# Gated MLP up to the token mix: from a fixed sequence after the planner to planned groups of four token tiles

## Chip, core, metric

One core of one Trainium2 chip. The metric is device time in microseconds (us), the median of the runs. The engines are TensorE (PE), VectorE (DVE), ScalarE (ACT), GpSimd (POOL) and SyncE (SP), which here issues nearly all DMAs. Each engine runs its instructions in the order in which the program emits them.

## What is computed

S = 2048 tokens, D = 640, Fh = 864, all in bfloat16. Cut to what matters:

```python
sa, ca, ga, sb, cb, gb = split(silu(c) @ w_mod)          # six rows of 640
h  = layernorm(x) * (1 + ca) + sa                        # x = A_q
kv = shift_conv(A_k, shift_k) * A_v                      # 4 taps
y  = irfft(rfft(kv, 2S) * rfft(ssm_k, 2S))[:S] + kv * ssm_D
x  = x + ga * (h * y)
h  = layernorm(x) * (1 + cb) + sb
z  = gelu(h @ w_in);  z1, z2 = z[:, :Fh], layernorm(z[:, Fh:])
g  = w_sp @ z2 + b_sp[:, None]                           # token mix, 2048 x 2048
out = x + gb * ((z1 * g) @ w_out)
```

## The kernel before

**Long convolution.** It is done as a transform by matrix products. The 640 channels are cut into four units (`UNITS`, L25: 128, 192, 192, 128 wide). For each unit the filter (`K`) and the data (`U`) are loaded as `X`, go through a first small transform (`stage1`, L377, PE then an ACT copy into `X1`), and then through 16 frequency blocks: the forward transform `pu` (L398; for the filter ACT copies it to `KH`, L415), the product `T` on DVE (L426), the inverse `pz` (L430, six matmuls) and an ACT copy into `Z` (L443). A block's tables are `M2` (forward; POOL, DVE and ACT sine, L318) and `G2` (inverse; PE transposes of `M2` and copies, L346). When a unit's `Z` is whole, it is transposed into `ZT`, by DMA (L602) or, for the last unit, on PE (L608). Then `py` (L573) gives `y`, which DVE multiplies into `gh`, the normalised and modulated `x` (L588, L592). `resid` (L626) adds `gh` to `xt` in four groups of four token tiles and takes the row statistics `st2`, per unit.

**Data.** `kv` is made strip by strip: two DMA transposes for `k` and `v` (`load_kv`, L452), four taps on PE, a DVE product (L485), and a store to `kv_scr` in DRAM (L488), from which a unit's `X` is loaded (L368). The modulation rows come through 18 loads `wm` (L522), with two buffers. POOL does `gh_mod` (L560), the residual adds of the first three units, and reciprocal roots (L193).

**Order.** All of this is recorded as operations with costs, dependencies and a wanted step `t` (`Plan`, L36). `run` (L60) repeatedly takes the operation that can start first by its cost model, among equals the one with the smallest `t`, and emits it. `SLOTS` (L33) gives the buffers of each tag; a DMA holds SP for its modelled transfer and lands `LAND` ns later. The steps `t` are written by hand in each call.

**MLP.** It is emitted after the planner, when the transform's pools are closed: `prep` (aggregate, root), `norm` (`xn`), `flip` (PE transposes of `xn`, modulated into `h2T`), 32 `z2` accumulations (L758) with Gelu on ACT and statistics on DVE, then 28 for `z1T` (L790), the normalisation of `z2` (L798), the token mix over all 16 tiles of `z2` (L809) and the output product (L821). `wT`, the transposed `w_sp`, is loaded by 16 DMA transposes (L715) into memory that `gh` and the transform's tiles held.

Of the kernel before, what the change touches and what calls it, by code (L numbers as in the profile page):

```python
# [10 lines left out]
ALU = mybir.AluOpType  # L11
# [18 lines left out]
WS = ((0, 256), (256, 256), (512, 128))  # L30
HOP = 150
LAND = 2000
SLOTS = dict(X=3, X1=3, KH=17, T=4, Z=2, ZT=2, wm=2, big=2, dg=2, st1=2, ga=1, s1=2, pu=3, pz=2, py=1)  # L33


class Plan:  # L36
# [6 lines left out]
    def op(self, eng, fn, r=(), w=(), t=0.0, new=()):  # L43

        i = len(self.ops)
        deps = set()
# [10 lines left out]
        self.ops.append(dict(eng=eng, fn=fn, deps=deps, t=t, new=new))  # L57
        return i

    def run(self, engines):  # L60
# [14 lines left out]
        held = {}  # L75
# [17 lines left out]
        while len(order) < len(ops):  # L93
            best = None
            for i in ready:
# [4 lines left out]
                for e, cost in o["eng"].items():  # L100
# [3 lines left out]
                    key = (max(at, free[e]), o["t"], i)  # L104
# [4 lines left out]
            (at, _, _), i, e, cost = best  # L109
# [5 lines left out]
            done[i] = at + cost + (LAND if e == "SP" else 0)  # L115
# [10 lines left out]
def kernel(  # L126
# [70 lines left out]
    w_in = {}  # L197
    with ExitStack() as actx:
        consta = actx.enter_context(tc.tile_pool(name="consta", bufs=1))
        gh = consta.tile([P, NT, D], BF16)  # L200
        M2 = consta.tile([P, 3, NKC, P], BF16)
        G2 = consta.tile([P, 4, NKC, P], BF16)
# [12 lines left out]
        rstd1 = consta.tile([P, NT], F32)  # L215
        F1flat = F1bd[:].rearrange("p j g -> p (j g)")
# [3 lines left out]
        tl = {}  # L220
# [3 lines left out]
        def new(name, tag, shape, dtype=BF16, pool=None):  # L224
            if pool is None:
                pool = psA if tag in ("s1", "pu", "pz", "py") else bigp if tag == "big" else apool
# [48 lines left out]
        def f1_table():  # L275
# [16 lines left out]
                gmask[:, None, :].to_broadcast([P, NJ, 8]), op=ALU.mult), w=["F1"], t=-50)  # L292


        def e_table():
            t = -4
# [3 lines left out]
            def angles(e):  # L300
# [17 lines left out]
        def m2_chunk(i):  # L318
            t = -34 + 2 * i
# [43 lines left out]
        def load_X(name, src, u, t, r=()):  # L363
# [491 lines left out]
```

## Time and profile before

| | |
|---|---|
| median of 3 runs | 378.61 us (378.11 to 378.89) |
| the profiled execution | 379.7 us, of which span 377.7 us |
| first inverse matmul, last inverse matmul | 44.53, 159.1 us |
| first `z2` matmul, first mix matmul | 181.5, 247.1 us |
| mean granted TensorE clock | 0.977 |

The span goes from the first to the last instruction. In a row of the timeline stand start, duration, engine, line, operation, out<-in and count, and in brackets the idle time ahead of it and what ended it. In a group's row stand count, busy time, mean ns, idle time ahead. A row of DMA issues ends with the median us from issue to landing. Several matmuls in one row overlap, so a row's duration holds one latency beside the array's own time. "SPq" is SP's DMA queue.

### The profile page before, as it was taken

The numbers are of one execution on the slowest core, as the hardware profiler recorded it, in microseconds if no ns is written. First come the engines' busy times: TensorE is split into PE (matmuls) and PEld (weight loads), VectorE is DVE, ScalarE is ACT, GpSimd is POOL, SyncE is SP. The second block draws the span as 40 slices with busy tenths as digits, with TensorE's granted clock in tenths as the row PEclk, the third lists the DMA queues.
The fourth block names the chain that finished last, engine by engine and source line by source line (L and its number), as shares of the span: only waits on it lengthen the run. The fifth ranks groups of instructions, "written<-read, shape, count | busy, mean of one in ns | idle before, by whom it ended". The sixth has DMA issues, their size and how long they took to land.

```text
span 377.7 us, 6095 instructions
## 1 busy us (share of the span) xinstructions
PE 331.1 (88%) x2394; PEld 203.7 (54%) x2394; DVE 228.6 (61%) x497; ACT 150.8 (40%) x318; POOL 113.8 (30%) x117
## 2 busy tenths in 40 slices
PE   1388699899999999821999999999999999999996
PEld 0136575668667788720555544444444444446774
DVE  7769899566737988897777669012333233234553
ACT  4467356858598586430766655510000000000000
POOL 8942320583829579062200078000000000000000
PEclk9999999999999999985799999999999999999999
DMA  9869929398995669705999901000000000000222
GB/s 122 240 150 218 247 81 192 122 203 140 169 239 116 159 185 194 112 0 109 222 233 191 256 2 24 4 2 0 4 12 0 14 2 0 0 2 29 86 82 83
DMA packets 112708, 40.08 MB, mean 106 GB/s; under 512 B 97992, under 2 KB 111912, under 8 KB 112680
## 3 DMA queue, kind: packets, MB, share of 16 engines
q1 hardware_dynamic: 111184, 39.18, 48.8%
q0 software_dynamic: 192, 0.52, 0.7%
q8 instruction: 18, 0.29, 0.3%
q10 hardware_dynamic: 1304, 0.00, 0.2%
q14 instruction: 10, 0.08, 0.1%
HBM read 16.63 MB, written 5.24 MB: 58 GB/s over the span
## 4 chain that ended last, share of the span: by engine, by line
PE 56%; DMA 3%; DVE 3%; issue 3%; POOL 1%; ACT 1%; ACTq 0%; DVEq 0%; POOLq 0%
PE ps L809 26%; PE ps L821 8%; PE ps L790 8%; PE ps L758 7%; PE pz L231 3%; DMA ZT<-Z 2%; PE pu L231 2%; PE tp L746 1%; DVE xn L740 1%; DMA wm<-in_w_mod_dram 1%; PE s L231 1%; POOL xt L630 1%; DVE st L633 1%; DVE T L426 1%; PE py L231 0%
## 5 line engine op out<-in xcount | busy, mean ns | idle before, releaser
L809 PE MATMUL ps<-wT,z 128*128 128x512 bf16 (+1 forms) x448 | 96.9, 379 | 0.0
L809 PEld LDWEIGHTS <-z 128*128 128x128 bf16 (+1 forms) x448 | 45.4, 101 | 51.3
L812 DVE TENSOR_TENSOR gt<-ps,bsp 128x512 bf16<-128x512 f32 (+1 forms) x28 | 19.3, 691 | 75.2 <-PE ps L809 75.2
L426 DVE TENSOR_TENSOR T<-pu,KH 128x512 bf16<-128x512 f32 (+1 forms) x64 | 50.6, 817 | 16.5 <-PE pu L231 9.2
L231 PE MATMUL pu<-X,M 128*128 128x128 bf16 (+3 forms) x384 | 49.8, 254 | 0.7 <-ACT KH L415 0.7
L231 PE MATMUL pz<-T,G 128*128 128x192 bf16 (+3 forms) x384 | 45.4, 255 | 3.1 <-DVE T L426 2.8
L393 ACT CAST X<-s 128x512 bf16<-128x512 f32 x80 | 43.9, 592 | 6.6 <-PE s L231 5.8
L231 PEld LDWEIGHTS <-G 128*128 128x128 bf16 x384 | 32.5, 98 | 10.6 <-issue 4.1
L231 PEld LDWEIGHTS <-M 128*128 128x128 bf16 x384 | 33.1, 97 | 9.3 <-issue 1.5
L231 PE MATMUL s<-big,dg 128*128 128x512 bf16 x80 | 22.9, 428 | 16.1 <-DMA big<-in_A_k_dram 8.4
L443 ACT CAST Z<-pz 128x256 bf16<-128x256 f32 (+1 forms) x64 | 27.2, 428 | 23.8 <-PE pz L231 22.2
L231 PE MATMUL s<-F1bd,X 128*128 128x256 bf16 x160 | 29.6, 277 | 5.0 <-ACT X L393 2.8
L758 PE MATMUL ps<-big,h2T 128*128 128x432 bf16 x160 | 31.9, 354 | 0.0
L821 PE MATMUL ps<-w_o,z1T 128*128 128x320 bf16 (+1 forms) x224 | 30.7, 299 | 0.0
L790 PE MATMUL ps<-h2T,big 128*128 128x512 bf16 (+1 forms) x140 | 30.4, 379 | 0.0
L415 ACT CAST KH<-pu 128x256 bf16<-128x256 f32 (+1 forms) x64 | 25.7, 432 | 11.6 <-PE pu L231 9.9
L821 PEld LDWEIGHTS <-z1T 128*128 128x128 bf16 (+1 forms) x224 | 21.8, 97 | 8.9
L762 DVE BATCH_NORM_STATS2 stz<-z 128x6 f32<-128x432 bf16 x32 | 19.3, 609 | 9.8 <-ACT z L761 9.7
L565 POOL TENSOR_TENSOR gh<-gh,gsa_bf 128x512 bf16<-128x512 bf16 (+1 forms) x16 | 22.3, 1396 | 9.0 <-DVE gsa_bf L551 8.0
L630 POOL TENSOR_TENSOR xt<-xt,gh 128x768 bf16<-128x768 bf16 (+1 forms) x12 | 17.5, 1489 | 23.7 <-DVE gh L592 23.7
L823 DVE TENSOR_TENSOR ot<-ps,xt 128x320 bf16<-128x320 f32 x32 | 15.7, 491 | 14.2 <-PE ps L821 14.2
L565 POOL TENSOR_TENSOR gh<-gh,gca_bf 128x512 bf16<-128x512 bf16 (+1 forms) x16 | 22.3, 1396 | 4.6 <-DVE gca_bf L546 4.6
(106 smaller groups left out, 356.6 us busy)
## 6 DMA issues: line engine op xcount, KB each, us to landing
wm<-in_w_mod_dram SPq DMA_DIRECT2D x12, 320.0 KB, 4.2
xt<-in_A_q_dram SPq DMA_DIRECT2D x2, 1280.0 KB, 6.7
kv_scr<-big SPq DMA_DIRECT2D x5, 512.0 KB, 3.4
out_dram<-ot SPq DMA_DIRECT2D x16, 160.0 KB, 1.8
big<-in_B_w_in_dram SPq DMA_DIRECT2D x2, 1080.0 KB, 7.3
X<-in_A_ssm_k_dram SPq DMA_DIRECT2D x2, 768.0 KB, 6.4
X<-kv_scr SPq DMA_DIRECT2D x2, 768.0 KB, 6.9
X<-in_A_ssm_k_dram SPq DMA_DIRECT2D x2, 512.0 KB, 5.5
```

What stands on the lines that cost most here:

```text
L231: nc.tensor.matmul(o, lhsT=w, rhs=x, start=start, stop=stop)
L393: e.copy(dst, tl[name][:].rearrange("p i (j g) -> p i j g", g=8))
L415: op({"ACT": act_cost(2 * du)}, lambda e: e.copy(tl[KH][:, :, 0:du], tl[pk][:, :, 0:du]), r=[pk], w=[KH], t=t)
L426: e.tensor_tensor(T_[:, :, :, 0:du], tl[pu][:, :, None, 0:du].to_broadcast([P, 2, 2, du]), tl[KH][:, None, :, 0:du].to_broadcast([P, 2, 2, ...
L443: op({"ACT": act_cost(2 * du)}, lambda e: e.copy(tl[Z][:, 0:du // 4, 2 * kc:2 * kc + 2, :], tl[pz][:, :, 0:du] .rearrange("p r (q c) -> p ...
L565: lambda e, vec=vec, o=o: e.tensor_tensor(gvu, gvu, vec[:, None, d0:d0 + du].to_broadcast([P, TB, du]), op=o),
L630: op(eng, lambda e: e.tensor_tensor(sl, sl, gh[:, g * TB:(g + 1) * TB, d0:d0 + du], op=ALU.add), r=[("gh", (u, g))], w=[("xt", (u, n)) for ...
L758: nc.tensor.matmul(ps[:, :FC], lhsT=h2T[:, kt, n * P:(n + 1) * P], rhs=w_in2[:, kt, fc * FC:(fc + 1) * FC], start=(kt == 0), stop=(kt == N ...
L762: nc.vector.bn_stats(out=stz[:, n, fc, :], in_=zsl)
L790: nc.tensor.matmul(ps[:fsz[ft], :], lhsT=w_in1[:, kt, ft * P:ft * P + fsz[ft]], rhs=h2T[:, kt, sc_i * TC:(sc_i + 1) * TC], start=(kt == 0) ...
L809: nc.tensor.matmul(ps[:fsz[ft], :], lhsT=z2[:, st_i, ft * P:ft * P + fsz[ft]], rhs=wT[:, st_i, tci * TC:(tci + 1) * TC], start=(st_i == 0) ...
L821: nc.tensor.matmul(ps[:, :HS], lhsT=z1T[:fsz[ft], ft, n * P:(n + 1) * P], rhs=w_o[:fsz[ft], ft, h * HS:(h + 1) * HS], start=(ft == 0), sto ...
```

## The change

- The MLP up to the token mix becomes part of the plan (`z_group`, four groups of four token tiles). A group's `h2T` and `z2` live in one tile `hz` that takes a slot of `X1` or, for the last group, of `Z`; its normalised rows take a slot of `Z`; its matmuls use the transform's PSUM slots `pu` and `pz`; `z1T` lies in the memory of `M2` and `G2`. Roots and normalisations are done per group.
- The wanted steps come from a table, `WANT`, one number for each kind of operation, found by a search on the planner's own model.
- The planner's model: a DMA transpose (`flip`) starts behind the landing of the transfer ahead of it and lands after half of `LAND`; DMA rates are new; `pz` may be taken out of program order; the row statistics, `xn` and the copies of the last unit may go to ACT or DVE.
- The modulation rows come in 14 loads with one buffer. `warm`, a Gelu of one column, is recorded ahead of the `M2` sines. Pools opened after the plan wait tile by tile.

```diff
+FIXED = ("X", "X1", "KH", "Z", "big", "ZT")
 HOP = 150
...
 LAND = 2000
-SLOTS = dict(X=3, X1=3, KH=17, T=4, Z=2, ZT=2, wm=2, big=2, dg=2, st1=2, ga=1, s1=2, pu=3, pz=2, py=1)
+SLOTS = dict(X=3, X1=3, KH=17, T=4, Z=2, ZT=2, wm=1, big=2, dg=2, st1=2, s1=2, pu=3, pz=2, py=1)
...
+WANT = {
+    "f1": -75.75, "m2": -37.25, "e": 23.75, "g2": -9, "sc": -167.5, "kv0": -97.75, "kv1": -148.25, "kv2": 29,
+    "kv3": 67.75, "kv4": 54.25, "taps0": -180.5, "taps1": -29.75, "taps2": -89, "taps3": 11, "taps4": 12.25,
...
+        t = WANT[lab] + off if lab else off
...
-                if tag in ("X", "X1", "KH", "Z", "big", "ZT", "pz"):
+                if tag in FIXED:
...
+                    at = max(at, free[e])
+                    key = (at, o["t"], i)
                     if best is None or key < best[0]:
-                        best = (key, i, e, cost)
+                        best = (key, i, e, cost, max(at, landed) if o["flip"] else at)
...
-            done[i] = at + cost + (LAND if e == "SP" else 0)
+            done[i] = at + cost
+            if e == "SP":
+                done[i] += LAND / 2 if o["flip"] else LAND
+                landed = at if o["flip"] else done[i]
...
+    span = ctx.enter_context(tc.tile_pool(name="span", bufs=1))
+    M2 = span.tile([P, 3, NKC, P], BF16)
+    G2 = span.tile([P, 4, NKC, P], BF16)
...
+    z1T = [(M2 if i < 3 else G2)[:, i % 3 if i < 3 else i - 3].rearrange("p k q -> p (k q)") for i in range(NFT)]
...
+                if e is nc.scalar:
+                    on_act.append(n)
+                    e.activation(gh[:, n, :], xt[:, n, :], ACT.Copy, accum_out=sums[:, n, 0:1])
+                    e.activation(gh[:, n, :], xt[:, n, :], ACT.Square, accum_out=sums[:, n, 1:2])
...
+            op(dma(400, 180), load, w=[wm], new=[(wm, "wm")], t=(t[0], -3))
...
+            step = 10 if u == NU - 1 else 1
...
+        op({"ACT": 1500}, lambda e: e.activation(warm[:], halfpi[:], ACT.Gelu_apprx_tanh), r=["M2", "e2c"], w=["warm"], t=("", 20))
...
+        op({"DVE": 1}, lambda e: new("xn2", "Z", [P, 2 * TB, D]), w=["xn2"], new=[("xn2", "Z")], t=("zp", 0))
+
+        def z_group(g):
+            t = 10 * g
+            ns = range(g * TB, (g + 1) * TB)
+            hz = "hz%d" % g
+            for n in ns:
+                op({"DVE": 250}, lambda e, n=n: e.bn_aggr(out=mv2[:, n, :], in_=st2[:, n, :, :]),
+                   r=[("st2", (u, n)) for u in range(NU)], w=[("mv2", n)], t=("zp", t))
+            op({"POOL": 1600}, lambda e: rstd_from_var(rstd2[:, ns[0]:ns[-1] + 1], mv2[:, ns[0]:ns[-1] + 1, 1]),
+               r=[("mv2", n) for n in ns], w=[("rs2", g)], t=("zp", t))
+            for n in ns:
+                op({"DVE": 500}, lambda e, n=n: e.tensor_scalar(tl["xn2"][:, n % (2 * TB), :], xt[:, n, :], mv2[:, n, 0:1],
+                                                                rstd2[:, n:n + 1], op0=ALU.subtract, op1=ALU.mult),
+                   r=[("mv2", n), ("rs2", g)] + [("xt", (u, n)) for u in range(NU)], w=[("xn2", n % (2 * TB))], t=("zx", t))
+            for dt in range(ND):
+                pt = "ft%d_%d" % (g, dt)
+
...
+                op(pe(*[128] * TB), flips, r=[("xn2", n % (2 * TB)) for n in ns], w=[pt], new=[(pt, "s1")], t=("zf", t))
+                op({"ACT": 780, "DVE": 600}, modulate, r=[pt, "sb", "cb"] + ([(hz, "new")] if dt else []),
+                   w=[(hz, dt)] + ([] if dt else [(hz, "new")]), new=[] if dt else [(hz, "X1" if g < 3 else "Z")], t=("zf", t))
...
+                    op(pe(*[FC] * ND), mul, r=[(hz, dt) for dt in range(ND)] + ["w_in1"], w=[ps], new=[(ps, tag)], t=("z2", t))
+                    op({"ACT": 540}, lambda e, ps=ps, zo=zo: e.activation(tl[hz][:, zo:zo + FC], tl[ps][:, :FC], ACT.Gelu_apprx_tanh),
+                       r=[ps], w=[(hz, ("z", i, fc))], t=("z2", t))
+                    op({"DVE": 620}, lambda e, n=n, fc=fc, zo=zo: e.bn_stats(out=stz[:, n, fc, :], in_=tl[hz][:, zo:zo + FC]),
+                       r=[(hz, ("z", i, fc))], w=[("stz", (n, fc))], t=("zs", t))
...
+            for ft in range(NFT):
...
+                op(pe(*[TC] * ND), mul1, r=[(hz, dt) for dt in range(ND)] + ["w_in0"], w=[ps], new=[(ps, tag)], t=("z1", t))
+                op({"ACT": 620}, lambda e, ft=ft, ps=ps: e.activation(z1T[ft][:fsz[ft], g * TC:(g + 1) * TC], tl[ps][:fsz[ft], :],
+                                                                      ACT.Gelu_apprx_tanh), r=[ps], w=["z1_%d_%d" % (g, ft)], t=("z1", t))
+
+        for g in range(NT // TB):
+            z_group(g)
...
+    wsp_pool = ctx.enter_context(tc.tile_pool(name="wsp", bufs=1, reuse_waits="tile"))
+    bwork = ctx.enter_context(tc.tile_pool(name="bwork", bufs=2, reuse_waits="tile"))
+    psB = ctx.enter_context(tc.tile_pool(name="psB", bufs=2, space=bass.MemoryType.PSUM, reuse_waits="tile"))
...
+    w_o = span.tile([P, NFT, D], BF16, tag="Z", bufs=SLOTS["Z"], name="w_o")
...
+        nc.gpsimd.tensor_tensor(w_o[:fsz[ft], ft, :], w_o[:fsz[ft], ft, :], gb_bf[:fsz[ft], :], op=ALU.mult)
...
+                zo = ND * TC + st_i % TB * Fh + ft * P
+                nc.tensor.matmul(ps[:fsz[ft], :], lhsT=tl["hz%d" % (st_i // TB)][:, zo:zo + fsz[ft]],
```

What this makes of the engines' queues is shown at three places. First SP at the program's start; `big` is a strip of `k` and `v`, `X<-in_A_ssm_k` a unit's filter, `X<-kv_scr` its data. Before:

```order
L459 DMA_TRANSPOSE big<-in_A_k_dram 128x2048
L368 DMA X<-in_A_ssm_k_dram 128x16x128
L461 DMA_TRANSPOSE big<-in_A_v_dram 128x2048
L459 DMA_TRANSPOSE big<-in_A_k_dram 128x2048
L494 DMA xt<-in_A_q_dram 128x8x640
L488 DMA kv_scr<-big 128x2048
L461 DMA_TRANSPOSE big<-in_A_v_dram 128x2048
L368 DMA X<-kv_scr 128x16x128
```

Now:

```order
L499 DMA_TRANSPOSE big<-in_A_k_dram 128x2048 x2
L501 DMA_TRANSPOSE big<-in_A_v_dram 128x2048 x2
L405 DMA X<-in_A_ssm_k_dram 128x16x128
L529 DMA kv_scr<-big 128x2048
L535 DMA xt<-in_A_q_dram 128x8x640
L405 DMA X<-kv_scr 128x16x128
```

Two strips are loaded ahead of everything; the filter, `xt` and the first store have moved behind them.

Second SP at the loads of units 1 and 2 (`X` 128x24x128), with the modulation loads `wm` between them. Before:

```order
L488 DMA kv_scr<-big 128x2048
L461 DMA_TRANSPOSE big<-in_A_v_dram 128x2048
L522 DMA wm<-in_w_mod_dram 128x5x256
L368 DMA X<-kv_scr 128x24x128
L522 DMA wm<-in_w_mod_dram 128x5x256 x2
L488 DMA kv_scr<-big 128x2048
```

Now:

```order
L535 DMA xt<-in_A_q_dram 128x8x640
L529 DMA kv_scr<-big 128x2048
L583 DMA wm<-in_w_mod_dram 128x5x320
L405 DMA X<-kv_scr 128x24x128
L405 DMA X<-in_A_ssm_k_dram 128x24x128
L583 DMA wm<-in_w_mod_dram 128x5x320
```

The first `wm` has moved ahead of this piece; the one that is shown first needs its buffer back, and unit 1's `X` stands behind it.

Third DVE from the last unit's residual adds on (`xt<-xt,gh`), with row statistics (`BN_STATS`), aggregates (`BN_AGGR`) and the normalised rows (`xn`, now in a slot of `Z`). Before:

```order
L630 TENSOR_TENSOR xt<-xt,gh 128x4x128
L633 BN_STATS st_72<-xt 128x6 x4
L734 BN_AGGR mv_2766<-st_72 128x2 x8
L740 TENSOR_SCALAR xn<-xt,mv_2766,rstd_2767 128x640 x4
L752 TENSOR_SCALAR h2T<-tp,cb_col,sb_col 128x512 x2
```

Now:

```order
L695 TENSOR_TENSOR xt<-xt,gh 128x4x128
L698 BN_STATS st_72<-xt 128x6 x4
L773 BN_AGGR mv_88<-st_72 128x2 x4
L695 TENSOR_TENSOR xt<-xt,gh 128x4x128
L698 BN_STATS st_72<-xt 128x6 x4
L773 BN_AGGR mv_88<-st_72 128x2
L698 BN_STATS st_72<-xt 128x6 x4
L773 BN_AGGR mv_88<-st_72 128x2
L778 TENSOR_SCALAR Z<-xt,mv_88,rstd_89 128x640 x4
L695 TENSOR_TENSOR xt<-xt,gh 128x4x128
L698 BN_STATS st_72<-xt 128x6 x5
L773 BN_AGGR mv_88<-st_72 128x2
```

Before, the piece that is shown begins with the last of four adds; now it begins with the first, and the first group's aggregates and normalised rows come ahead of the third group's add. The fourth stands 37 rows further down than the third, behind the normalisations of the first group's `z2`.

More of the change, by code (lines that the diff above doesn't have):

```diff
@@ L56, in op @@
                 seen.append((i, part, wr))
[L57 removed]
+        self.ops.append(dict(eng=eng, fn=fn, deps=deps, t=t, new=new, flip=flip))
         return i
@@ L215 @@
         rstd1 = consta.tile([P, NT], F32)
+        nmr1 = consta.tile([P, NT], F32)
+        sums = consta.tile([P, NT, 2], F32)
+        on_act = []
+        warm = consta.tile([P, 1], F32)
         F1flat = F1bd[:].rearrange("p j g -> p (j g)")
@@ L754, in z2_tile @@
-    def z2_tile(n):
-        for fc in range(NFC):
-            ps = psB.tile([P, 512], F32, tag="mm", bufs=5, name="ps")
-            for kt in range(ND):
-                nc.tensor.matmul(ps[:, :FC], lhsT=h2T[:, kt, n * P:(n + 1) * P],
-                                 rhs=w_in2[:, kt, fc * FC:(fc + 1) * FC], start=(kt == 0), stop=(kt == ND - 1))
-            zsl = z2[:, n, fc * FC:(fc + 1) * FC]
-            nc.scalar.activation(zsl, ps[:, :FC], ACT.Gelu_apprx_tanh)
-            nc.vector.bn_stats(out=stz[:, n, fc, :], in_=zsl)
```

414 lines of the change are left out of this document (201 added, 213 removed), and 9 rows, old and new, of the table WANT.

## Prediction

> **What bounds the kernel now.** First the page's head and TensorE (PE)'s sums, then the stages that the chain of waits suggests, cut at PE's first and last inverse-transform matmul (`pz`), its first MLP-up matmul (`z2`) and its first token-mix matmul.
>
> ```profile
> span 377.7 us, 6095 instructions
> PE 331.1 (88%) x2394; PEld 203.7 (54%) x2394; DVE 228.6 (61%) x497; ACT 150.8 (40%) x318; POOL 113.8 (30%) x117
> 0.00:44.50 44.50, 24.58 (x149) 13.50 (x150) 34.66 (x99) 23.44 (x53) 26.98 (x46) 1.00 0.90 195
> 44.50:159.10 114.60, 107.47 (x1126) 84.09 (x1126) 86.56 (x164) 80.59 (x187) 59.32 (x47) 1.00 0.79 162
> 159.10:181.60 22.50, 6.99 (x93) 5.52 (x91) 18.30 (x59) 5.02 (x7) 9.23 (x8) 0.66 0.33 69
> 181.60:247.10 65.50, 64.81 (x362) 33.54 (x360) 42.22 (x89) 41.17 (x70) 17.18 (x15) 0.99 0.64 126
> 247.10:377.70 130.60, 127.28 (x673) 67.06 (x670) 46.89 (x88) 0.59 (x1) 1.09 (x2) 1.00 0.07 23
> ```
>
> Columns: stretch, its length, busy time of PE, weight loads, VectorE (DVE), ScalarE (ACT), GpSimd (POOL), then granted clock, DMA share, GB/s. The last two stages are PE without a gap. The third is a hole of 22.5 us with 7.0 us of PE work. The second is full at first sight, but a matmul's record covers its latency too. The mix gives the rate of a full array:
>
> ```profile
> 247.13 96.69 PE ps L809 x448
> ```
>
> That is 96.69/448 = 216 ns per 512 columns. Counting the columns of all matmuls between first and last `pz` in the two orders at that rate gives 97.6 us before and 98.0 us after. So the second stage holds 17 us in which PE streams nothing, and the first holds 44.5 - 16.4 = 28 us by the same count.
>
> Next the rows of the start: PE's first `pz`, and what came before it.
>
> ```profile
> 22.08 0.34 SPq L488 DMA_DIRECT2D kv_scr<-big  x1
> 25.32 0.51 SPq L368 DMA_DIRECT2D X<-kv_scr  x1
> 17.02 1.28 DVE L485 TENSOR_TENSOR big<-s,big 128x512 bf16<-128x512 f32 x2
> 43.80 4.33 DVE L426 TENSOR_TENSOR T<-pu,KH 128x512 bf16<-128x512 f32 x7
> 44.53 0.60 PE L231 MATMUL pz<-T,G 128*128 128x256 bf16 x6 [1.31 <-DVE T L426]
> ```
>
> The first `kv` strip went out at 22.08, since DVE multiplied its four pieces from 17.02 on only, between `M2` chunks. Unit 0's first product stood at 43.80 on a DVE without idle time, behind eight row statistics, seven normalisations and three `G` copies.
>
> Last, the hole, in order of time: the last two `pz` groups, a piece of the chain of waits, DVE's last multiplies and residual adds, the reciprocal roots, the first `z2`.
>
> ```profile
> 158.03 1.05 PE L231 MATMUL pz<-T,G 128*128 128x256 bf16 x12
> 166.76 8.51 issue
> 168.02 0.66 DVE L592 TENSOR_TENSOR gh<-gh,py 128x512 bf16<-128x512 bf16 x1
> 169.66 0.40 DVE L630 TENSOR_TENSOR xt<-xt,gh 128x512 bf16<-128x512 bf16 x1
> 170.09 0.87 DVE L633 BATCH_NORM_STATS2 st<-xt 128x6 f32<-128x128 bf16 x4
> 174.58 1.10 DVE L734 BATCH_NORM_AGGREGATE mv<-st 128x2 f32<-128x24 f32 x8
> 175.71 1.02 POOL L195 TENSOR_TENSOR rstd<-rstd,mhalf 128x4 f32<-128x4 f32 x1
> 176.77 1.51 DVE L740 TENSOR_SCALAR xn<-xt,mv,rstd 128x640 bf16<-128x640 bf16 x4 [1.09 <-POOL rstd L195]
> 181.45 3.01 PE L758 MATMUL ps<-big,h2T 128*128 128x432 bf16 x10
> ```
>
> All four groups' residual adds and statistics (169.66 to 174.6) and eight aggregates stand ahead of the first group's root. The chain's 8.51 us of "issue" from 166.76 is this DVE work, on whose result POOL waits.
>
> **The change part by part.** I add four stages up: first `pz`, last `pz`, first `z2`, first mix matmul.
>
> *Start.* Both `k` and both `v` strips now load first, and DVE's multiplies of strip 0 stand right after `M2` chunk 1, not behind the chunks 2 and 3, for which DVE waited on POOL. Four back-to-back transposes of 512 KB: the `wT` row below gives 37.21/16 = 2.33 us each, so `v0`, now third, lands by about 13; four taps and multiplies end near 16.5, and `kv_scr` goes out there and not at 22.08. `xt` (6.7 us) and unit 0's `X` (5.8 us after the 3.4 us of the store) then land near 24 and 26.
>
> ```profile
> L501 DVE BATCH_NORM_STATS2 st<-xt 128x6 f32<-128x320 bf16 x32 | 13.8, 474 | 0.0
> L502 DVE BATCH_NORM_AGGREGATE mv<-st 128x2 f32<-128x12 f32 x16 | 3.3, 209 | 0.6
> L355 DVE COPY G<-s 128x1024 bf16<-128x1024 bf16 x4 | 2.7, 672 | 0.0
> xt<-in_A_q_dram SPq DMA_DIRECT2D x2, 1280.0 KB, 6.7
> kv_scr<-big SPq DMA_DIRECT2D x5, 512.0 KB, 3.4
> X<-kv_scr SPq DMA_DIRECT2D x2, 512.0 KB, 5.8
> ```
>
> In DVE's new order seven tiles' statistics, 7 x (2 x 0.474 + 0.209) = 8.1 us, the last `M2` chunk and four copies, 2.7 us, stand ahead of the first product, and the normalisations behind it: 24 + 12 = 36, so first `pz` about 37 (36 to 44.5, the upper end being no gain). Against it, `warm` is a Gelu that now runs before the sine tables' `M2` work, and adds two table loads on ACT:
>
> ```profile
> 2.84 1.28 ACT L265 ACT_TABLE_LOAD   x1 [2.84 <-DVE f1k L285]
> 4.14 0.32 ACT L265 ACTIVATE f1c<-fr,halfpi 128x32 f32<-128x32 f32 x1
> 8.13 0.42 ACT L336 ACTIVATE M<-T 128x256 bf16<-128x256 f32 x1 [2.15 <-DVE T L333]
> ```
>
> Two loads cost 2 x 1.28 = 2.6 us; ACT waited 2.15 us there for DVE, so about 0.5 us shows, plus the `e2c` sine that now stands ahead of `M2`. That delays the first `M2` chunks by 2 to 3 us; the statistics that stand behind are what hides it, and uncovered it is 3 us. [...]
>
> *Second stage.* The same 64 products and `pz` groups, in another order. At before's rate 98.0 us of array time take 98.0 x 114.6/97.6 = 115 us; without any gap they take 98. I take 111: the long breaks between units, where DVE had no product (the 4.11 us ahead of unit 1, the 3.77 us ahead of unit 2), are what an order can close; the short gaps within units are latencies of PE, DVE and ACT in turn, and I leave them.
>
> ```profile
> 78.44 2.69 DVE L426 TENSOR_TENSOR T<-pu,KH 128x768 bf16<-128x768 f32 x3 [4.11 <-PE pu L231]
> 114.39 1.82 DVE L426 TENSOR_TENSOR T<-pu,KH 128x768 bf16<-128x768 f32 x2 [3.77 <-ACT KH L415]
> L393 ACT CAST X<-s 128x512 bf16<-128x512 f32 x80 | 43.9, 592 | 6.6 <-PE s L231 5.8
> ```
>
> Two tiles' statistics move to ACT (about 0.7 us for each of four passes, an estimate from 0.6 us for 512 columns in L393's 592 ns): ACT has 34 us idle in this stage, so nothing, at most 2.8 us. Last `pz` at 37 + 111 = 148 (135 to 159.5).
>
> *Hole.* No `z2` matmul comes ahead of the last `pz`: its row statistics need all four units. What changes is that group 0 goes alone. Ahead of its root stand one residual add, four statistics, four aggregates, 0.40 + 0.87 + 0.55 = 1.8 us, where 169.66 to 175.68 held 6.0: minus 4.2. DVE then does group 1's add, eight statistics and two aggregates, 2.5 us, while POOL takes 1.3 us: plus 1.2. Unit 1's statistics, formerly inside the second stage, now stand between the last multiplies (18 statistics there for 16): plus 0.5. So 22.5 - 4.2 + 1.7 = 20 us (16 to 23); z2 at 168.
>
> *MLP up.* Same matmuls; PE was busy 64.8 of 65.5 us. The new order puts ten flips of group 2 behind 26 us of matmuls, with DVE's own queue there about 24.6 us long: 1 us for a near miss, 66.5 (65.5 to 69). The mix begins at 234.5. Its operands: `wT` waits for the last residual add, which now stands on DVE behind group 0's normalisations.
>
> ```profile
> 173.96 37.21 SPq L715 DMA_TRANSPOSE wT<-in_B_w_sp_dram  x16
> wT<-in_B_w_sp_dram SPq DMA_TRANSPOSE x16, 4.7
> L762 DVE BATCH_NORM_STATS2 stz<-z 128x6 f32<-128x432 bf16 x32 | 19.3, 609 | 9.8 <-ACT z L761 9.7
> L798 DVE TENSOR_SCALAR z<-z,mvz,rstdz 128x864 bf16<-128x864 bf16 x16 | 14.3, 969 | 3.3 <-POOL rstdz L195 3.3
> ```
>
> From the first `z2` DVE has 16 x 0.609 + 5 x 0.969 = 14.6 us of these, four modulations, four `xn` and some statistics, about 22 us, before it. Release to last landing took 173.75 to 213.8 = 40 us, so `wT` is whole 62 us after the first `z2`, 4.5 us before it is read: cost nothing. `bsp` loads later too, behind `w_o`; the mix's six PSUM buffers, 6 x 3.45 us, cover that.
>
> *Sum.* 37 + 111 + 20 + 66.5 + 130.6 (mix and output unchanged) = 365.1 us of span. The profiled run took 379.7 at a span of 377.7, so 367.1; it lay 1.1 above the median of 378.61, so 366.0.
>
> **Rivals.**
> *Order closes the second stage* (101 us for 111): 356. For it: 17 us of empty array. Against: DVE's 86.6 and ACT's 80.6 us of work run in turn with PE.
> *Second stage gives the start back* (last `pz` near 159): 377. For it: DMA share 0.79 there; loads that come no earlier hold units 1 to 3 where they were.
> *`wT` late.* Each us by which the last residual add slips beyond 26 us after the first `z2` is a us of the mix; slipping to 31 gives 371. Against: 4.5 us of cover. [...]
> *Slower: the single `wm` buffer.* Each of the 14 modulation loads now waits on SP until PE has used the one before, and four of unit 1 to 3's `X` loads stand straight behind such a load.
>
> ```profile
> wm<-in_w_mod_dram SPq DMA_DIRECT2D x12, 320.0 KB, 4.2
> X<-kv_scr SPq DMA_DIRECT2D x2, 768.0 KB, 6.9
> ```
>
> A place fully exposed costs PE 4.2 + 6.9 = 11 us; it decides from 366 + 12.6, that is a little over one place. Two give 388. Against: PE has some 10 us of other matmuls between the `wm` matmul and the first use of that `X`.
>
> **Numbers.** A measurement of this kernel can tell 0.2%, 0.8 us. Chances: forecast (360 to 372) 0.46, second stage closed 0.21, given back 0.12, `wT` late 0.07, these all faster, 0.86; no change 0.04; slower 0.10. Range 354 to 379: it takes in the closed stage and the given-back one, and leaves out the slower tail and little below.
>
> **What would show it.** After: first `pz` near 37, last near 148, first `z2` 20 us later, the mix 66.5 us after that without a wait for DMA `wT`, the mix and output 130.6 us again. Wrong if SP's rows show `X` loads issued later than before relative to their unit, if PE waits for `X` or `wm` by DMA for several us, if the last `pz` stands past 155, or if the mix waits for `wT`.

## The result and the profile after

| | before | after |
|---|---|---|
| median, us | 378.75 (378.11 to 380.24, 4 runs) | 363.32 (362.64 to 363.97, 4 runs) |
| profiled run, us | 379.7 | 363.97 |
| its span, us | 377.7 | 362.2 |

The ratio is 0.9587 (0.955 to 0.9623): 15.4 us less, where 366.0 was forecast. The same stages as in the prediction, cut at the changed kernel's own marks (first `pz` matmul, end of the last, first z2, first mix, end); columns are window, length, then busy time and instruction count of PE, weight loads, DVE, ACT and POOL, and last the granted clock, DMA share and GB/s:

```profile
0.00:38.96 38.96, 23.50 (x137) 12.22 (x138) 30.80 (x90) 26.01 (x55) 25.40 (x47) 0.96 0.93 190
38.96:147.70 108.74, 105.34 (x1110) 82.97 (x1108) 84.40 (x152) 81.79 (x194) 60.94 (x55) 1.00 0.83 182
147.70:167.10 19.40, 7.79 (x102) 5.98 (x99) 19.06 (x56) 6.98 (x11) 9.65 (x7) 0.72 0.01 3
167.10:231.38 64.28, 64.28 (x362) 33.60 (x360) 41.99 (x108) 37.88 (x66) 11.87 (x16) 0.98 0.72 148
231.38:362.20 130.82, 127.25 (x672) 67.05 (x670) 46.71 (x88) 0.59 (x1) 9.26 (x10) 1.00 0.08 25
```

Against before's 44.50, 114.60, 22.50, 65.50 and 130.60: the start gave 5.5 us, the second stage 5.9, the hole 3.1, the MLP 1.2, and the tail took 0.2. The start, the second stage and the hole moved the way the sum had it; the MLP, for which it had 1 us more, became shorter. PE's own idle time fell from 114.60 - 107.47 = 7.1 to 3.4 us in the second stage; in the MLP it is nil. In the hole DVE is busy 19.06 of 19.40 us. DVE and POOL there, from their timelines:

```profile
150.14 8.38 POOL L695 TENSOR_TENSOR xt<-xt,gh 128x768 bf16<-128x768 bf16 x5 [3.41 <-DVE gh L656]
...
160.66 1.02 POOL L218 TENSOR_TENSOR rstd<-rstd,mhalf 128x4 f32<-128x4 f32 x1
```
```profile
149.98 1.39 DVE L698 BATCH_NORM_STATS2 st<-xt 128x6 f32<-128x192 bf16 x5
...
152.02 1.63 DVE L652 TENSOR_TENSOR gh<-gh,wm 128x512 bf16<-128x512 bf16 x1
153.58 0.67 DVE L656 TENSOR_TENSOR gh<-gh,py 128x512 bf16<-128x512 bf16 x1
154.18 1.65 DVE L698 BATCH_NORM_STATS2 st<-xt 128x6 f32<-128x192 bf16 x6
155.74 1.28 DVE L652 TENSOR_TENSOR gh<-gh,wm 128x512 bf16<-128x512 bf16 x1
...
157.66 1.14 DVE L695 TENSOR_TENSOR xt<-xt,gh 128x512 bf16<-128x512 bf16 x1
158.84 0.87 DVE L698 BATCH_NORM_STATS2 st<-xt 128x6 f32<-128x128 bf16 x4
159.63 0.61 DVE L773 BATCH_NORM_AGGREGATE mv<-st 128x2 f32<-128x24 f32 x4
160.16 0.36 DVE L695 TENSOR_TENSOR xt<-xt,gh 128x512 bf16<-128x512 bf16 x1
...
162.66 1.45 DVE L778 TENSOR_SCALAR Z<-xt,mv,rstd 128x640 bf16<-128x640 bf16 x4
```

As forecast, group 0's one add, four statistics and four aggregates stand alone ahead of the root, 157.66 to 160.24, where all four groups' stood before, 169.66 to 175.68. Not forecast: the same 128x512 add takes 1.14 us at 157.66 and 0.36 at 160.16, and the multiplies L652 take 1.63 and 1.28 us, while POOL's five residual adds run beside the first add and both multiplies. The kernel before had two such multiplies, unseen by the prediction; the second, short as it is, began while POOL's last add still ran, to 166.76:

```profile
160.17 6.59 POOL L630 TENSOR_TENSOR xt<-xt,gh 128x768 bf16<-128x768 bf16 x4 [9.62 <-DVE gh L592]
```
```profile
162.25 1.44 DVE L588 TENSOR_TENSOR gh<-gh,wm 128x512 bf16<-128x512 bf16 x1 [0.16 <-ACT wm L586]
...
166.42 0.63 DVE L588 TENSOR_TENSOR gh<-gh,wm 128x512 bf16<-128x512 bf16 x1
```

### The profile page after: what moved, and what is told of

It is laid out like the page before. It is cut to its first block, busy times and chain, and to the rows that moved or that the text cites. A ratio compares the mean times of both kernels' runs of the same rounds, so it can differ in the third digit from the quotient of the medians.

```text
span 362.2 us, 6081 instructions
## 1 busy us (share of the span) xinstructions
PE 328.2 (91%) x2374; PEld 201.8 (56%) x2374; DVE 223.0 (62%) x492; ACT 153.3 (42%) x324; POOL 117.1 (32%) x133
## 4 chain that ended last, share of the span: by engine, by line
PE 82%; DVE 7%; ACT 6%; POOL 2%; DMA 1%; issue 1%; POOLq 0%; DVEq 0%; ACTq 0%
PE ps L863 27%; PE pu L269 19%; PE pz L269 16%; PE s L269 9%; PE ps L875 8%; ACT X L430 4%; DVE st L698 1%; PE s L787 1%; DMA ZT<-Z 1%; POOL T L366 1%; PE py L269 1%; DVE gh L652 1%; PE pu L680 1%; POOL T L365 1%; DVE T L465 0%
## 5 line engine op out<-in xcount | busy, mean ns | idle before, releaser
L863 PE MATMUL ps<-wT,X 128*128 128x512 bf16 (+1 forms) x336 | 77.1, 379 | 0.0
L863 PEld LDWEIGHTS <-X 128*128 128x128 bf16 (+1 forms) x336 | 34.1, 101 | 38.4
L269 PE MATMUL pu<-X,M 128*128 128x128 bf16 (+3 forms) x384 | 48.6, 254 | 1.1 <-ACT KH L453 1.1
L269 PEld LDWEIGHTS <-X 128*128 128x128 bf16 x280 | 26.4, 100 | 21.8 <-issue 10.4
L863 PE MATMUL ps<-wT,Z 128*128 128x512 bf16 (+1 forms) x112 | 28.7, 379 | 0.0
L877 DVE TENSOR_TENSOR ot<-ps,xt 128x320 bf16<-128x320 f32 x32 | 15.7, 491 | 14.2 <-PE ps L875 14.2
L875 PE MATMUL ps<-w_o,G 128*128 128x320 bf16 (+1 forms) x128 | 22.7, 299 | 0.0
L269 PEld LDWEIGHTS <-big 128*128 128x128 bf16 (+1 forms) x140 | 14.1, 102 | 15.2
L269 PEld LDWEIGHTS <-dg 128*128 128x128 bf16 x80 | 8.5, 108 | 21.6 <-issue 8.8
```

The costliest lines, as they stand in the source:

```text
L269: nc.tensor.matmul(o, lhsT=w, rhs=x, start=start, stop=stop)
L863: nc.tensor.matmul(ps[:fsz[ft], :], lhsT=tl["hz%d" % (st_i // TB)][:, zo:zo + fsz[ft]], rhs=wT[:, st_i, tci * TC:(tci + 1) * TC], start=(s ...
L875: nc.tensor.matmul(ps[:, :HS], lhsT=z1T[ft][:fsz[ft], n * P:(n + 1) * P], rhs=w_o[:fsz[ft], ft, h * HS:(h + 1) * HS], start=(ft == 0), sto ...
L877: nc.vector.tensor_tensor(ot[:, h * HS:(h + 1) * HS], ps[:, :HS], xt[:, n, h * HS:(h + 1) * HS], op=ALU.add)
```

## Experiments

All twelve start from the changed kernel. Where an edit is given as an order, the planner's finished order is kept and only the named steps are moved in it, each on its own engine. "Hole" below is the start of the last `pz` matmul to the first z2 matmul (19.6 us by these marks in the changed kernel, 22.6 before). Marks and medians, us:

| kernel | first pz | last pz | z2 | mix | span | median |
|---|---|---|---|---|---|---|
| changed | 39.0 | 147.3 | 166.9 | 231.2 | 362.2 | 363.32 |
| the same again (e12) | 37.8 | 146.1 | 165.6 | 229.7 | 360.6 | 363.30 |
| e1 strip 0 late | 41.5 | 149.8 | 169.4 | 234.4 | 365.3 | 367.39 |
| e2 all adds ahead | 37.9 | 146.2 | 168.5 | 232.2 | 363.1 | 365.41 |
| e3 statistics later | 38.8 | 147.1 | 165.8 | 241.2 | 372.1 | 374.18 |
| e4 and POOL later | 38.9 | 147.3 | 168.4 | 244.6 | 375.5 | 375.89 |
| e5 POOL gated | 37.9 | 146.2 | 162.2 | 227.1 | 358.1 | 359.77 |
| e6 old steps | 42.3 | 155.5 | 175.8 | 239.4 | 370.4 | 372.17 |
| e7 w_o first | 38.1 | 146.4 | 166.0 | 231.0 | 378.6 | 381.90 |
| e8 X first | 37.8 | 149.5 | 169.0 | 233.6 | 364.5 | 366.09 |
| e9 warm late | 38.7 | 147.0 | 166.6 | 230.8 | 361.7 | 363.30 |
| e10 gated, statistics | 38.2 | 146.5 | 162.4 | 226.5 | 357.4 | 359.21 |
| e11 gated, w_mod too | 37.1 | 145.5 | 161.2 | 225.6 | 356.6 | 358.44 |

The same program's first `pz` moved by 1.3 us between two profiles, and stood between 37.1 and 39.0 us in all kernels with the changed kernel's start (all but e1, e6 and e9), so single marks are read to about that, and stages (a difference of two marks of one profile) more finely. The nine runs of the changed kernel, e12's included, lie between 361.93 and 363.97 us.

The MLP stage holds one thing more: the clock granted to PE. In the changed kernel it is 0.5 from 156.3 to 170.0 us and 1.0 from there to 361.1, so the first 3.1 us of the MLP run at half the clock, where a `z2` matmul takes 0.56 us for 0.35. This share differs from run to run (1.8 us in e2, 4.4 in e5, 1.7 in e10), and differences of some tenths in that stage come with it.

**Which part brought what: the old steps (e6).**

```diff
+WANT.update({"f1": -50, "m2": -34, "kv0": -60, "kv1": -30, "taps0": -50, "taps1": -16, "XK0": -45, "XU0": -40,
...
+    "zt3": 67, "y3": 67, "res1": 44, "res2": 60, "res3": 76, "st1": 45, "st2": 61, "st3": 77})
```

> The changed kernel with the wanted steps of the spectral part set to those that the formulas of the kernel before give; the steps of the MLP, the planner's new costs, the single wm buffer and the wider modulation loads stay. Theory (the searched steps made the start and the second stage, the grouping made the hole): first pz at 43 to 45, last pz at 157 to 160, hole 19 to 20.5 us, z2 to mix 64 to 66 us: 374 to 376 us. Rival (the new planner and the wider loads shorten the second stage by themselves): last pz at or under 154, 367 to 371 us. Second rival (the single wm buffer costs where the steps were not searched for it): SP stands on wm, PE waits for X by DMA for several us, last pz beyond 161, over 377 us.

The time was 372.17 us, ratio to before 0.9832 (0.9802 to 0.9862). The start is 42.3, the second stage 113.2, the hole 20.3, z2 to mix 63.6. So the searched steps are worth 8.9 us of the 15.4, nearly all in the start (3.2 to 4.5) and the second stage (113.2 against 108.3); the rest, 6.6 us, comes with the planner's other costs, the wider loads and the grouping, which this run does not separate. Time and last `pz` (155.5) fell between the figures of the theory and of the first rival, which was half right: the new structure alone shortens start and stage by some 3 us. PE waited for no X, so the single `wm` buffer did no harm here either.

**Does the start pass through (e1)?**

```diff
 DVE: M2 chunk 1
-DVE: 4 multiplies of strip 0 (L526), between the chunks 1 to 3
 DVE: M2 angles of chunk 3
+DVE: 4 multiplies of strip 0 (L526)
```

> The changed kernel with one edit of its finished order: DVE's four multiplies of strip 0, and the two tap groups that wait for their PSUM buffers, stand behind the angles of M2 chunk 3, where the kernel before had them, and not right after chunk 1. Everything else keeps its order. Theory (the start's gain passes through): kv_scr goes out at 21 to 22 us instead of 16.88, the first pz comes at 43 to 44 instead of 39.0, and last pz, first z2 and first mix each come 4 to 5 us later; 367 to 368 us. Rival (the second stage takes up what the start loses, since units 1 to 3 do not hang on it): first pz as above, but last pz at 147 to 149 and 363 to 365 us. Second rival (the store is not what the first pz hangs on; DVE's row statistics are): first pz at most 1.5 us later, and 363 to 365 us.

The store's row on SP, of the changed kernel and of this one:

```profile
16.88 0.34 SPq L529 DMA_DIRECT2D kv_scr<-big  x1
```
```profile
21.10 0.34 SPq L545 DMA_DIRECT2D kv_scr<-big  x1
```

The store went out 4.2 us later; the first `pz` came 2.5 us later, less than the 4 to 5 expected. Against the repeated profile, whose store went out at 15.03, it is 6.1 and 3.7 us. So the first `pz` follows the store only in part. First `pz` to last is 108.3 us in both, and the median rose by 4.1 to 367.39 (367.11 to 367.86), ratio 0.9677 (0.9618 to 0.9736). The second stage takes nothing up: what the start wins reaches the end.

**The hole: group 0 alone (e2).**

```diff
+DVE: residual adds and statistics of unit 3, groups 1, 2, 3
 DVE: 4 aggregates of group 0
 POOL: root of group 0
-DVE: residual adds and statistics of unit 3, groups 1, 2, 3 (spread behind)
```

> The changed kernel with one edit of its finished order: the residual adds of groups 1 to 3 and their twelve row statistics stand on DVE ahead of group 0's aggregates, as in the kernel before. Theory (the hole is DVE's queue, and group 0 alone ahead of its root is what shortened it): 3 x 0.38 + 12 x 0.22 = 3.8 us more stand ahead of the root, of which about 1.2 us had stood in the root's shadow: the hole grows from 19.4 to about 22 us, the time to about 366 us (365 to 367). Rival (the MLP takes it back, since DVE has that much less to do later): the hole grows alike, but the stage from first z2 to first mix falls below 64 us and the time stays within 0.8 us of 363.3. Second rival (PE, ACT and DVE wait for each other in turn and DVE's queue is not the bound): the hole stays at 19.4 to 20 us.

The hole grew from 19.6 to 22.3 us and the time to 365.41 (364.95 to 365.69), ratio 0.962 (0.957 to 0.9669): 2.8 and 2.1 us more, the theory's 366 to 0.6 us. z2 to mix fell from 64.3 to 63.7, as much as the shorter share at half the clock explains (1.8 us for 3.1), so nothing shows that the MLP took anything back.

**The hole: which of DVE's work (e3, e4, e5, e10, e11).** In e3 the statistics of later groups leave the hole; to feed DVE, PE's order in the MLP is changed as well:

```diff
-DVE: 14 statistics of units 1 and 2, groups 1 to 3, ahead of group 0's normalisations
+DVE: the same, behind group 0's modulations
-PE: flips of group 1 between z2 matmuls 4 and 7; z2 of group 1, then z1 of group 0
+PE: flips of group 1 behind z2 matmul 7; z1 of group 0, then z2 of group 1
```

> The changed kernel, finished order edited: row statistics of units 1 and 2 that belong to groups 1 to 3 (ten ahead of group 0's root, some behind it) stand behind group 0's modulations, group 1's flips stand two z2 groups later on PE, and group 0's z1 matmuls go ahead of group 1's z2 to give DVE the time. Theory (DVE's queue is the hole): ten statistics at 0.24 us leave it, so the hole falls from 19.4 to about 17 us (16.5 to 17.5) and the time to about 361 us, if no new wait comes up in the MLP. Rival (the statistics only fill waits of DVE for py, ACT and PE, one after the other through the single py buffer): the hole stays at 18.7 to 19.4 us, the time at 362.5 to 363.5. Second rival (group 1 comes late): the hole shrinks but PE waits for group 1's Z or X by DVE, and the stage from z2 to mix grows by 1 to 3 us.

The time rose to 374.18 us, ratio 0.9862 (0.9807 to 0.9916). The hole fell by 0.9 us only, and PE then stood in the MLP, its longest waits from the last `pz` on:

```profile
PE s L810 <- DVE Z L801: 9.8, 2, 6.5
PE s L810 <- DVE X L819: 3.0, 1, 3.0
```

Of the first row 6.5 us are the hole itself; the other 3.3 and the 3.0 are new, and z2 to mix took 75.4 us, 11.1 more. Beside these 6.3 us the clock fell to 0.5 twice more (179.7 to 183.1, 203.6 to 207.0). The theory failed; each rival held in its mechanism and neither in its figures. The ten statistics ahead of the first residual add won nothing: from the last `pz` to that add it is 10.3 us with them and without, since DVE now waits where they had stood. The 0.9 us came behind the root, where four statistics and two aggregates had kept the normalisations waiting.

```profile
149.12 0.69 DVE L679 TENSOR_TENSOR gh<-gh,py 128x512 bf16<-128x512 bf16 x1 [0.84 <-PE py L292]
151.47 0.69 DVE L708 COPY ZT<-pu 128x1024 bf16<-128x1024 bf16 x1 [1.66 <-ACT gb_bf L624]
```

The stall in the MLP is my own reordering's doing, and says nothing of the change. e4 besides moves POOL's last adds behind the root:

```diff
-POOL: res1 g0-2, res2 g0, g1, g2, g3, res1 g3, root g0
+POOL: res1 g0-2, res2 g0, root g0, res2 g1, g2, g3, res1 g3
```

> The kernel of the statistics moved later, and besides POOL's last four residual adds (units 1 and 2, groups 1 to 3) stand behind group 0's root on POOL, so that they do not run beside DVE's multiplies of the last unit. Theory (a POOL stream beside them slows DVE's bf16 operations: the multiply of gh by the copied y took 1.63 and 1.28 us with POOL busy and 0.63 us in the kernel before with POOL idle, the first residual add 1.14 us against 0.36): these three fall to 0.63, 0.63 and 0.4 us, minus 2.4 us, less up to 1 us that the normalisations of group 0 may now lose to the same contention; 1.4 to 2.4 us off the hole against the kernel of the statistics moved later, 359 to 360 us. Rival (the long times are something else, such as the PSUM or the buffer that ACT writes): the three keep 1.0 to 1.6 us, and the time stays within 0.8 us of that kernel.

DVE (two multiplies, then the normalisations) and POOL in e4:

```profile
152.24 0.41 DVE L676 TENSOR_TENSOR gh<-gh,wm 128x512 bf16<-128x512 bf16 x1
...
154.35 0.43 DVE L676 TENSOR_TENSOR gh<-gh,wm 128x512 bf16<-128x512 bf16 x1
...
158.86 6.78 DVE L802 TENSOR_SCALAR Z<-xt,mv,rstd 128x640 bf16<-128x640 bf16 x4 [0.29 <-POOL rstd L242]
```
```profile
158.80 6.65 POOL L719 TENSOR_TENSOR xt<-xt,gh 128x768 bf16<-128x768 bf16 x4
```

The multiplies fell to 0.41 and 0.43 us, and the slowing came back on the normalisations: four took 6.78 us for 1.45, beside POOL's four adds of 6.65. So the hole grew to 21.2 us and the time to 375.89, ratio 0.9908 (0.988 to 0.9937). The theory was right on the mechanism and far too low on its price there (up to 1 us expected, 5.3 found). Its 0.63 us "with POOL idle" was no undisturbed price either: POOL's add beside it ended at 166.76, and with POOL idle beside it the multiply takes 0.42 in e5. e5 keeps the changed kernel's PE order and holds POOL back until the normalisations are through:

```diff
-POOL: res1 g0-2, res2 g0, g1, g2, g3, res1 g3, root g0, root g1
+POOL: res1 g0-2, res2 g0, root g0, copy of xn2[3], res2 g1, root g1, copy of xn2[7], res2 g2, g3, res1 g3
-DVE: statistics of unit 2 as in the changed kernel
+DVE: those of groups 1 to 3, and group 1's aggregates, behind the modulations of group 0
```

> The changed kernel; PE's order is untouched. On POOL, unit 2's residual adds of groups 1 to 3 and unit 1's of group 3 stand behind group 0's root, and a copy of one element of the normalised group 0 stands ahead of the first of them (of group 1, ahead of the second), so that no add can run beside DVE's last multiplies, its residual add or its normalisations. The statistics that need these adds stand later on DVE. Theory (a POOL stream holds DVE's all-bf16 operations until its own operation is through): the two multiplies take 0.4 us instead of 1.63 and 1.28, the first residual add 0.4 instead of 1.14, the normalisations of group 0 keep 0.4 us each; the hole falls from 19.4 to 16.5 us (16 to 17.5), the stage after it keeps 64 to 65 us, and the time is 360 to 361 us. Rival (the hole is set by other waits, as of DVE for py and of PE for the flips): the hole falls by under 1 us. Second rival (the later adds make group 1 late): PE waits for Z by DVE inside the MLP, and the stage from z2 to mix grows by 1 to 3 us.

```profile
150.91 0.42 DVE L674 TENSOR_TENSOR gh<-gh,wm 128x512 bf16<-128x512 bf16 x1
...
153.15 0.42 DVE L674 TENSOR_TENSOR gh<-gh,wm 128x512 bf16<-128x512 bf16 x1
...
154.51 0.42 DVE L721 TENSOR_TENSOR xt<-xt,gh 128x512 bf16<-128x512 bf16 x1
...
157.85 1.52 DVE L805 TENSOR_SCALAR Z<-xt,mv,rstd 128x640 bf16<-128x640 bf16 x4 [0.29 <-POOL rstd L239]
```

All four rows are short again. From the last `pz` to z2 it is 15.9 us, 3.6 less, z2 to mix takes 65.0, and the time is 359.77 (358.31 to 360.04), ratio to before 0.9484 (0.9458 to 0.951): 3.5 us under the changed kernel, just under the theory's 360 to 361. The 3.6 us have two parts. From the last `pz` to the first residual add it is 8.3 us for 10.3, which is the two multiplies, and the add itself is 0.7 us shorter: 2.8 us by keeping POOL away. The other 0.9 us lie behind that add and are those that e3 had won, by the statistics and aggregates that left the place ahead of the normalisations. On this base e10 moves eight statistics of unit 1 out of the hole, and e11 also the last two modulation matmuls and their casts off the head of unit 3's `py` chain:

```diff
-DVE: statistics of unit 1, groups 1 and 2, between the last multiplies
+DVE: group 1's behind group 0's normalisations, group 2's behind group 0's z statistics
```

> The gated kernel, and eight statistics of unit 1 (groups 1 and 2), which stood on DVE between the last multiplies, stand behind group 0's normalisations (group 1's four, where DVE waits 1.83 us for the flips) and behind group 0's row statistics of z (group 2's four). Theory (with POOL out of the way DVE's queue is the hole's bound): 8 x 0.24 = 1.9 us leave it, the hole falls by 1 to 1.9 us from 16.0, and the time by as much from 359.8, to 358 to 359. Rival (the last unit's chain through the single py buffer, PE to ACT to DVE and back, is the bound, and the statistics filled its waits): the hole falls by under 0.5 us.

```diff
-PE: ... py2, flips of unit 3, mod50, py3    ACT: casts of gb, y copy
+PE: mod51, py2, mod50, flips of unit 3, py3    ACT: y copy, casts of gb
```

> The kernel before this one, and besides the last two modulation matmuls (w_mod 5) earlier on PE and the load between them earlier on SP, so that they do not stand ahead of the last unit's first py matmuls, and ACT's casts of them behind its first y copy. Theory (0.84 us of matmul and 0.42 us of cast leave the path to the first y copy): another 0.7 to 1.2 us off the hole, 357 to 358 us. Rival (DVE's queue sets the hole, not the first py): within 0.4 us of the kernel before this one. Second rival (the modulation matmuls now wait on PE for their loads): last pz 1 to 2 us later and 359 to 361 us.

In e10 the hole is 15.9 us and the time 359.21 (ratio 0.9479, 0.9451 to 0.9507). The hole did not move, which is the rival: the statistics had filled waits. In e11 the hole is 15.7 us, 0.2 less where the theory had 0.7 to 1.2, and the time 358.44 (0.9469, 0.9441 to 0.9496), the fastest of all. But its interval overlaps those of e5 and e10, and 0.8 us of its lead over e5 is its first `pz`. That anything beyond e5 helps is not shown.

**`wT` (e7).**

```diff
+    (w_o: allocation, 7 loads, 7 multiplies)
     for st_i in range(NT):
         nc.sync.dma_start_transpose(wT[:, st_i, :], B_w_sp[:, st_i * P:(st_i + 1) * P])
-    (w_o: allocation, 7 loads, 7 multiplies)
```

> The changed kernel with the loads of w_o ahead of those of wT on SP's queue. w_o takes the buffer of the normalised groups and so waits for the last flips of group 3, at about 204.5 us; wT, behind it, then starts at about 208 and not at 188.3 us. Theory (wT's last landing comes 40.4 us after its first issue, 228.6 now, and its last tile is read 3.2 us into the mix at 234.4): the last landing moves to 248 to 249, the mix's first sum waits for it, and the time grows by about 14 us to 376 to 379 us. Rival (the load goes faster when it starts later, as it runs beside fewer other transfers): under 10 us more. Second rival (the mix can wait, since the sums behind have slack): under 3 us more.

SP's rows of `wT` in the changed kernel and in e7, and PE's waits in the mix of e7:

```profile
188.27 37.63 SPq L850 DMA_TRANSPOSE wT<-in_B_w_sp_dram  x16
```
```profile
209.31 37.83 SPq L854 DMA_TRANSPOSE wT<-in_B_w_sp_dram  x16
```
```profile
PE ps L863 <- DMA wT<-in_B_w_sp_dram: 12.8, 8, 1.9
```

The load began 21.0 us later and took as long as before, 37.8 us for 37.6; the span grew by 16.4 us, the median by 18.6 to 381.90, ratio 1.0081 (1.0057 to 1.0105). The theory's mechanism stands, its 376 to 379 us were 3 us low. In the changed kernel the last of the sixteen is issued at 223.5 and lands at 227.9; it is first read 15 x 0.216 us into the mix, at 234.4, so 6.5 us were free. In e7 it lands at 249.4, 21.5 us later, and 21.5 - 6.5 = 15.0 us show in the span. The rest goes with the clock: between the waits it is 0.5, from 235.3 to 252.4 us, and until then a mix matmul took up to 0.63 us for 0.38.

**The single `wm` buffer (e8).**

```diff
-SP: wm, X of unit 1 (u); wm, X of unit 2 (u); wm, X of unit 3 (k); wm, X of unit 3 (u)
+SP: X, wm; X, wm; X, wm; X, wm
```

> The changed kernel with unit 1 to 3's X loads (four of them) ahead of the modulation load that stood straight before each on SP's queue, so that no X load waits for the single wm buffer. Theory (the single buffer costs nothing here, since PE waits for X by DMA for 0.0 us in the second stage and for wm 0.5 us): last pz within 1 us of 147.3 and the time within 1 us of 363.3. Rival (X behind the waiting wm load costs): last pz 2 to 6 us earlier, 357 to 361 us. Second rival (the modulation loads, now behind, come late for the multiplies): last pz or the hole grows, 364 to 367 us.

PE's waits for `wm` in the second stage, changed kernel and e8:

```profile
PE s L269 <- DMA wm<-in_w_mod_dram: 0.5, 1, 0.5
```
```profile
PE s L288 <- DMA wm<-in_w_mod_dram: 3.5, 3, 1.7
```

The time is 366.09, ratio 0.9678 (0.963 to 0.9725): 2.8 us slower, which is the second rival. With X ahead, it is the modulation loads that PE waits for, and first `pz` to last takes 111.7 us for 108.3. No X load was late to begin with: in the changed kernel PE has no wait for X by DMA. What a second `wm` buffer would give was not run.

**The two table loads (e9).**

```diff
-ACT: Silu, warm (Gelu), sines
+ACT: Silu, sines, ..., last y copy of the hole, warm (Gelu)
```

> The changed kernel with the one-column Gelu (warm) on ACT behind its last y copy of the hole instead of ahead of the sines, so that ACT loads Sin, Silu, Sin early, three tables and not four, and Gelu in the hole. Theory (the early loads are hidden: DVE's first angles end at 8.7 us, 1.3 us before the first M2 sine at 10.02, and DVE's row statistics stand behind): the first M2 sine comes at 8.7 to 9.2 us, first pz stays at 37.5 to 39, and the time within 0.8 us of the changed kernel's 363.3. Rival (the two loads, 2.6 us, are on the path): kv_scr and first pz 2 to 3 us earlier, 360 to 361 us. [...]

```profile
5.99 1.28 ACT L711 ACT_TABLE_LOAD   x1
7.29 0.20 ACT L711 ACTIVATE warm<-halfpi 128x1 f32<-128x1 f32 x1
7.51 1.28 ACT L303 ACT_TABLE_LOAD   x1
...
10.02 0.40 ACT L373 ACTIVATE M<-T 128x256 bf16<-128x256 f32 x1
```
```profile
5.76 0.21 ACT L722 ACTIVATE sc<-c_bf 128x5 f32<-128x5 bf16 x1
9.79 0.31 ACT L319 ACTIVATE e2c<-fr,halfpi 128x16 f32<-128x16 f32 x1 [3.82 <-DVE fr L313]
10.00 0.40 ACT L389 ACTIVATE M<-T 128x256 bf16<-128x256 f32 x1
```

The first fence is the changed kernel, the second e9. Both loads are gone (the sine behind Silu needed none), and ACT waits 3.82 us for DVE instead, at the `e2c` sine that stands ahead of `M2`. So the first `M2` sine comes at 10.00 for 10.02, not at 8.7 to 9.2 as expected, and the time is 363.30, ratio 0.9584 (0.9557 to 0.9611). The loads cost nothing here. Behind the load ahead of `warm` there is no gap: 5.99 + 1.28 = 7.27, and `warm` starts at 7.29.

**The changed kernel again (e12).**

> The changed kernel itself once more, beside the three above: 363.3 us, within 0.8 us, with the marks of its own profile within 1.2 us.

The time is 363.30, ratio 0.958 (0.955 to 0.9611). The marks of its profile are 1.3 to 1.5 us earlier, a little more than expected.

## Why the prediction was right, and where it was not

The time was forecast as 366.0 us and came out 363.3. In the span the terms were off by +2.0 (start), -2.3 (second stage), -0.6 (hole), -2.2 (MLP) and +0.2 us (tail), -2.9 in all; that the first two cancel is luck.

*Start*, 37 forecast, 39.0 and 37.8 measured. The path was the one named: `kv_scr` went out at 16.88 (forecast 16.5), `xt` landed at 24.0 and unit 0's `X` at 26.3 (24 and 26), and the first product (37.86) stood on a DVE without idle time just ahead of it. Too small was the last term: from the landing of `xt` to the first product it is 13.9 us, not 12. The charge of 0.5 us for `warm` was too much; e9 finds 0.

*Second stage*, 111 forecast, 108.7 measured. The size was near and the reason given was wrong. The step failed that took the long breaks between units, where DVE had no product, for what an order can close. Ahead of unit 1 the break is nearly what it was (3.54 us for 4.11), the one ahead of unit 2 closed (0.34 for 3.77), and a new one of 4.61 us stands inside unit 1, at its ninth product:

```profile
71.57 3.55 DVE L465 TENSOR_TENSOR T<-pu,KH 128x768 bf16<-128x768 f32 x4 [3.54 <-PE pu L269]
...
91.36 1.96 DVE L465 TENSOR_TENSOR T<-pu,KH 128x768 bf16<-128x768 f32 x2 [4.61 <-PE pu L269]
...
108.24 0.96 DVE L465 TENSOR_TENSOR T<-pu,KH 128x768 bf16<-128x768 f32 x1 [0.34 <-PE pu L269]
```

That is 8.5 us of breaks for 7.9, and the stage is 5.9 us shorter. What shrank is PE's idle time, 7.1 to 3.4 us, and its busy time, by 2.1. PE works through DVE's breaks: it is busy in all of the 4.61 us and in 2.7 of the 3.54. e6 shows the reverse: there the breaks ahead of units 1 and 2 are 2.70 and 1.06 us, PE is idle for 8.1 us, and the stage is 4.9 us longer than in the changed kernel. PE is now busy 105.34 of 108.74 us, so an order has 3.4 us left to close by this count; whether the 98.0 us of array work from which the rival of 101 us was made can be reached, no run shows.

*Hole*, 20 forecast, 19.4 measured. It is read in two parts, cut at the first residual add of the last unit. From the last `pz` to that add the sum had 0.5 us more, for two more statistics; it became 0.5 shorter (10.8 to 10.3), although POOL's adds cost the two multiplies 1.63 + 1.28 - 2 x 0.42 = 2.1 us, of which the kernel before had paid 1.44 + 0.63 - 2 x 0.42 = 1.2. The statistics there cost nothing, as e3 and e10 show; what else shortened this part was not tested by itself. From the add to the first `z2` the sum had 4.2 - 1.2 = 3.0 us less, for group 0 alone ahead of its root; it became 2.5 shorter (11.8 to 9.3), with 0.7 us lost on the add beside POOL, and e2 gives 2.8 us for this step. So the step holds, POOL's 2.8 us were not in the sum, and the two parts miss it by 1.0 and 0.5 us in opposite directions.

*MLP*, 66.5 forecast, 64.3 measured, below the low end of 65.5. The near miss for group 2's flips did not come; PE waits for nothing there. The 0.7 us of idle time before went too, which the low end had kept.

*`wT`*: cost nothing, as forecast; it is whole at 227.9, 3.3 us before the mix begins, where the sum had 4.5. The tail of 130.6 came out 130.8.

*Rivals.* Second stage closed: it came to 108.7 us and not 101. Start given back: refuted by e1; the `X` loads of units 1 to 3 did come earlier, at 53.9, 87.5 and 99.2 us for 56.9, 94.0 and 111.8. `wT` late: not here, and e7 gives its price. Single `wm` buffer: PE waits 0.5 us for `wm` in the second stage and never for `X` by DMA, and e8, which puts `X` ahead of the waiting load, is slower.

## What to carry to other kernels

Read a stage that PE bounds from PE's idle time first: here DVE's breaks were as long after the change as before (8.5 us for 7.9), and the stage was 5.9 us shorter, since PE had other work to run through them. An early gain is worth its full length only if the stages behind keep their lengths, which one delayed step tests directly. A busy engine is not yet the bound: DVE was busy 19.06 of the hole's 19.40 us, and taking ten statistics from it ahead of the first residual add won nothing. Before leaving elementwise work on POOL, look at what runs on DVE beside it: here the adds that looked free cost DVE 2.8 us, and holding them back was worth more than moving any statistic.

## What the runs showed of the hardware

Three kinds of DVE's operations on SBUF tiles, bf16 in and out by their rows, took longer beside a residual add of POOL and ended behind it. The residual add took 1.14 us, 0.36 without POOL; the multiply of `gh` by the copied `y` (L652) 1.63 and 1.28 us, 0.42 in e5; and in e4 four normalisations took 6.78 us beside four adds of 6.65, and 1.45 in the changed kernel. There the two multiplies and the add ended 0.28 to 0.29 us behind the POOL add beside them (153.66, 157.03 and 158.80 for 153.37, 156.75 and 158.52). Statistics (154.18, 0.28 us each) and multiplies with an operand from PSUM (L656, 0.67 us) keep their times beside the same adds (0.28 and 0.69 in e5, without them). What makes the one kind wait and the other not, no row shows.

In these profiles the clock granted to PE is 0.5 in some stretches and 1.0 in the others. In the changed kernel it fell at 156.3 us, inside the hole, and came back at 170.0, 3.1 us after the first `z2`; in e7 it fell at 235.3 us among the waits for `wT` and came back at 252.4, 2.9 us after the last of them. In both, the matmuls behind the wait ran at half the clock (a `z2` matmul took 0.56 us for 0.35, a mix matmul up to 0.63 for 0.38), so the wait cost more than its own length.
